# Moving the softmax over slots ahead of the last stage, masking expert rows in the ReLU, six more landing places for expert weights, and a new order of work

## The chip, the core and the metric

The kernel runs on one core of one Trainium2 chip. The core has a matmul engine (TensorE, PE in the profile, with its weight loads shown apart as PEld), a vector engine (VectorE, DVE), an activation engine (ScalarE, ACT), a general engine (GpSimd, POOL) and a sync engine (SyncE, SP), which issues all the DMA transfers here. Each engine runs its own instructions strictly in the order in which they were written, and waits where data or a buffer is not ready. The metric is device time in microseconds, smaller is better.

## The reference

Three parts in a row: attention through 32 memory slots, a max-of-three feed-forward layer, and a soft mixture of 8 experts with 4 slots each. All in float32.

```python
# q, k, v: (8, 8, 576, 64); phi: (8, 8, 576, 32)
a = softmax(phi, over the sequence axis)
k_m = einsum('bhsm,bhsd->bhmd', a, k);  v_m = einsum('bhsm,bhsd->bhmd', a, v)
attn = softmax(q @ k_m.T / 8, axis=-1) @ v_m
x = attn.transpose(0, 2, 1, 3).reshape(4608, 512)
x = maximum(maximum(x @ w1, x @ w2), x @ w3) @ w_out          # 512 -> 768 -> 512
logits = x @ phi2                                              # (4608, 32)
d = softmax(logits, axis=0);  slot_input = d.T @ x             # (32, 512)
for e in range(8): slot_out[e] = maximum(slot_input[e] @ e_w1[e], 0) @ e_w2[e]   # 512 -> 1024 -> 512
c = softmax(logits, axis=1);  out = c @ slot_out
```

The first softmax of the mixture runs over all 4608 tokens and feeds the experts; the second runs over the 32 slots of each token ("the softmax over slots") and is needed only when the output is formed.

## The kernel before, in words

**Main phase.** The kernel treats 8 batches `n`, each with 6 blocks `i` of 128 hidden features: 48 units. A unit needs 6 groups `mn u hf r` (two halves `hf` of the tokens, three weight matrices `r`) of 6 matmuls each, at L641, written into one of three PSUM banks `m`. The function `ev` takes each group out: `r` 0 is a copy on ACT (L651), `r` 1 and 2 are maxima on DVE (L653, L655). Around the groups stand the small steps of the attention: maxima of phi (`mxr`, L426), exponentials, the sums over the sequence (`km`, L477; `kmr`, `kmc`), a transpose (`kvtm`, L501; `kvtc`, L505), scores (`scm`, L516; `sct`, L522), their softmax (`s1r` to `s3l`), and the products of memory and weights (`v1m`, L603; `v1h`, L617; `v1l`, L623). Hidden features are transposed by tokens through DRAM (`trm`, L692; `trc`, L707), multiplied into logits (`lg`, L722) and into running slot sums (`slm`, L789; `sla`, L801). The tokens left over at the end of each batch go the same way in one bundle (`rtm`, L815 and L817; `rtc`, L820; `rsm`). The weights of the feed-forward layer come as 64-bit words and are put together on three engines (`raw`, `cva` at L352, `cvb` at L356, `cvd` at L361, `cvp` at L366).

All of this is one hand-made list, `ORDER`: one pass over it writes the instructions of every engine and every DMA, so the list fixes what stands ahead of what in each engine's queue. `SLOTS` names the buffer that each step takes.

**Expert weights.** They are 64 pieces of 512 KB. `send` issues the next piece into the next of `NSLOT` = 44 places in SBUF; a place that was used is taken again by the piece 44 later. 38 pieces are sent in `ORDER`, the others by the code behind it: one when the main phase ends, one and four more as buffers come free, and the last 20 (44 to 63) while the experts run.

**Last stage.** After `ORDER` come the logits and sums of the last block, the slot inputs (L963 to L995), and the experts: `ex_in` (32 matmul records, L1065), a ReLU on ACT (L1070), `ex_turn` on DVE (a transpose, L1073, and a copy of the expert's four rows into a zeroed buffer `msk`, L1074), `ex_out` for the first half of the output (16 records, L1082). Between the experts, `work[e]` computes the softmax over slots in three pieces (`c_first`, L1020 to L1023; `c_second`, L1029 to L1033) and splits the result into a high part `ch` and a low part `cl`. Then come the 18 output tiles of 512 KB, `st_out` (L1126 to L1138), each with four PSUM copies and a DMA. The first 8 of half 0 alternate with `ex_out(r, 1)`, the second half of the experts' output:

```python
        so_a(0)
        ex_out(0, 1)
        so_b(0)
        for r in range(1, E):
            ex_out(r, 1)
            if r <= NH:
                st_out(r - 1, 0)
        so_a(1)
        st_out(NH, 0)
        so_b(1)
        st_out(NH + 1, 0, True)
```

`warm(n)` issues `n` matmuls that compute nothing, in places where PE would wait; `W` says how many stand at five places of the last stage.

Of the kernel before, what the change touches and what calls it, by code (L numbers as in the profile page):

```python
# [1217 lines left out]
```

## Time and profile before

| | us |
|---|---|
| median of 3 runs | 436.54 (435.85 to 437.97) |
| the profiled execution: its own time | 436.33 |
| the profiled execution: span from the first to the last instruction | 434.6 |

The profiled execution is 0.2 us under the median, and 1.7 us of its time lie outside the span. The granted TensorE clock was 0.991 of full speed over the span. Times below are counted in us from the span's start. Three points order the span: the first of the L641 matmuls at 24.85, the last of them at 363, and the first expert matmul at 378.8.

### The profile page before, as it was taken

The page shows a single profiled execution, that of the slowest core. Times are in us where ns is not written, and L with a number is a line of the kernel's source. Part 1 is how long each engine was busy: PE and PEld are TensorE (multiplying, and loading weights), DVE is VectorE, ACT ScalarE, POOL GpSimd, SP SyncE. Part 2 cuts the span into 40 slices and gives each one's busy share as a digit, 9 for nine tenths or more (in the row PEclk, how much of TensorE's full clock was granted, in tenths as well). Part 3 has the DMA queues.
Part 4 walks back from the last instruction along what each step waited for, and adds up shares of the span by engine and source line. Part 5 has one row for each costly group of instructions (what it writes and reads, how often), then busy time and mean ns, then how long its engine had stood idle before and what let it go on. Part 6 is the DMA issues. An engine that isn't in the chain of part 4 may idle for free.

```text
span 434.6 us, 12284 instructions
## 1 busy us (share of the span) xinstructions
PE 413.8 (95%) x5067; PEld 336.6 (77%) x5067; DVE 313.1 (72%) x731; ACT 182.4 (42%) x430; POOL 88.8 (20%) x102
## 2 busy tenths in 40 slices
PE   8989998999999999999999999999999999999990
PEld 8668787887888879888878798878988888555570
DVE  1597997577988887987599669888866544488480
ACT  3679583644535242344352434334332133132370
POOL 0356633351412011213022212020110000011000
PEclk9999999999999999999999999999999999999996
DMA  8999689928775684672758859468599998599997
GB/s 308 418 414 349 241 322 243 387 83 275 226 177 191 221 307 134 213 286 97 235 190 286 284 194 350 147 196 327 187 293 343 331 314 288 154 410 406 411 399 309
DMA packets 56072, 118.92 MB, mean 274 GB/s; under 512 B 8016, under 2 KB 32336, under 8 KB 53968
## 3 DMA queue, kind: packets, MB, share of 16 engines
q1 hardware_dynamic: 56016, 118.14, 76.9%
q8 instruction: 40, 0.66, 0.6%
q14 instruction: 16, 0.13, 0.1%
HBM read 96.49 MB, written 21.63 MB: 272 GB/s over the span
## 4 chain that ended last, share of the span: by engine, by line
PE 71%; DMA 12%; DVE 9%; ACT 3%; issue 1%; SPq 1%; POOL 1%; DVEq 0%; ACTq 0%; POOLq 0%
PE m L641 44%; DMA arena<-in_w_dram 7%; PE x L603 7%; PE x L477 3%; PE x L789 2%; DMA arena<-in_phi_n_dram 2%; PE m L1065 2%; PE x L1126 2%; PE l L722 2%; PE m L1082 2%; PE x L516 2%; DMA hbuf<-rt 1%; PE l L1082 1%; DMA rt<-arena 1%; DVE vl L623 1%
## 5 line engine op out<-in xcount | busy, mean ns | idle before, releaser
L641 PE MATMUL m<-ah,vh 128*128 128x288 f32 x504 | 147.5, 307 | 1.8 <-DVE g L653 1.1
L641 PE MATMUL m<-ah,vl 128*128 128x288 f32 x504 | 142.1, 296 | 0.0
L641 PEld LDWEIGHTS m<-ah,vh 128*128 128x128 f32 x504 | 94.6, 188 | 20.1 <-issue 11.3
L641 PE MATMUL m<-al,vh 128*128 128x288 f32 x504 | 107.8, 295 | 0.5 <-POOL al L573 0.3
L641 PEld LDWEIGHTS m<-ah,vl 128*128 128x128 f32 x504 | 94.7, 188 | 1.1 <-DVE vl L623 0.8
L641 PEld LDWEIGHTS m<-al,vh 128*128 128x128 f32 x504 | 80.6, 188 | 0.9 <-POOL al L573 0.9
L651 ACT ACTIVATE g<-m 128x288 f32<-128x288 f32 x96 | 39.3, 410 | 91.8 <-PE m L641 88.5
L653 DVE TENSOR_TENSOR g<-m,g 128x288 f32<-128x288 f32 x96 | 42.5, 445 | 26.4 <-PE m L641 16.2
L655 DVE TENSOR_TENSOR ht<-m,g 128x288 f32<-128x288 f32 x96 | 42.3, 451 | 11.6 <-PE m L641 9.1
L617 ACT ACTIVATE vh<-x 128x384 fp32r<-128x384 f32 (+1 forms) x88 | 36.5, 475 | 25.5 <-PE x L603 19.1
L623 DVE TENSOR_TENSOR vl<-x,vh 128x384 fp32r<-128x384 f32 (+1 forms) x88 | 42.5, 524 | 5.5 <-ACT vh L617 5.5
L603 PE MATMUL x<-w,kvt 64*32 64x384 f32 (+1 forms) x800 | 40.0, 477 | 0.9 <-POOL w L366 0.5
L573 POOL TENSOR_TENSOR al<-arena,ah 128x576 fp32r<-128x576 f32 x16 | 23.0, 1435 | 63.4 <-ACT ah L569 56.0
L366 POOL TENSOR_TENSOR w<-w,arena 128x768 uint32<-128x768 uint32 (+1 forms) x13 | 23.6, 1817 | 32.1 <-ACT km L496 15.0
L464 POOL TENSOR_TENSOR arena<-arena,bc 128x640 f32<-128x640 f32 x12 | 19.5, 1637 | 47.1 <-DMA bc<-bcd 22.4
L692 DVE STREAM_TRANSPOSE arena<-ht 128x512 f32<-128x512 f32 x30 | 20.8, 700 | 3.4 <-DMA tr<-arena 2.8
L641 PE MATMUL m<-ah,wh 128*128 128x288 f32 x72 | 21.2, 309 | 0.7 <-DVE ht L655 0.7
L603 PEld LDWEIGHTS x<-w,kvt 64*32 64x32 f32 x800 | 12.0, 105 | 12.3 <-issue 8.1
L641 PE MATMUL m<-ah,wl 128*128 128x288 f32 x72 | 20.2, 295 | 0.0
L801 DVE SCALAR_TENSOR_TENSOR s_run<-s_run,sm,x 128x384 f32<-128x384 f32 (+1 forms) x18 | 10.8, 603 | 9.0 <-PE x L789 9.0
L662 POOL COPY arena<-ht 128x64 f32<-128x64 f32 x24 | 5.3, 236 | 56.2 <-DVE ht L655 55.5
L665 POOL COPY hr_last<-ht 128x64 f32<-128x64 f32 x12 | 3.2, 275 | 66.5 <-DVE ht L655 66.5
(265 smaller groups left out, 649.2 us busy)
## 6 DMA issues: line engine op xcount, KB each, us to landing
arena<-in_e_w_dram SPq DMA_DIRECT2D x33, 512.0 KB, 6.9
arena<-in_w_dram SPq DMA_DIRECT2D x14, 768.0 KB, 7.8
hbuf<-tr SPq DMA_DIRECT2D x42, 256.0 KB, 5.2
arena<-in_kv_dram SPq DMA_DIRECT2D x8, 1290.0 KB, 7.9
arena<-in_q_dram SPq DMA_DIRECT2D x16, 576.0 KB, 7.4
arena<-in_kv_dram SPq DMA_DIRECT2D x8, 1032.0 KB, 7.4
tr<-arena SPq DMA_DIRECT2D x30, 256.0 KB, 2.4
arena<-in_phi_t_dram SPq DMA_DIRECT2D x8, 576.0 KB, 5.8
```

What stands on the lines that cost most here:

```text
L366: (eng or nc.gpsimd).tensor_tensor(out=du, in0=du, in1=lo.bitcast(U32), op=ALU.add)
L464: nc.gpsimd.tensor_tensor(out=x, in0=x, in1=bc_sb[:, :, b].unsqueeze(1).to_broadcast([128, 5, 128]), op=ALU.subtract)
L477: nc.tensor.matmul(t[32 * g:32 * g + 32, 0:KVC], phin_sb[:, j, b, 32 * g:32 * g + 32], kv_sb[:, j, b, g], start=(j == 0), stop=False, tile ...
L573: nc.gpsimd.tensor_tensor(out=al[n][:, :, c], in0=aT_sb[:, :, c], in1=ah[n][:, :, c].bitcast(FP32), op=ALU.subtract)
L603: nc.tensor.matmul(t[b][32 * g:32 * g + 32, 128 * r0:128 * r1], kvt[n][r, b, 32 * g:32 * g + 32], w_v[i][r, g, r0:r1], start=True, stop=Tr ...
L617: nc.scalar.activation(out=v1[n, i][0][:, b, c], in_=ph["v1", n, i, r0][b][:, c], func=ACTF.Copy)
L623: nc.vector.tensor_tensor(out=vl[:, b, c], in0=ph["v1", n, i, r0][b][:, c], in1=vh[:, b, c].bitcast(FP32), op=ALU.subtract)
L641: nc.tensor.matmul(t[:, 0:HALF], x, y, start=(k == 0), stop=(k == 5))
L651: nc.scalar.activation(out=g1[u, hf], in_=t[:, 0:HALF], func=ACTF.Copy)
L653: nc.vector.tensor_tensor(out=g1[u, hf], in0=t[:, 0:HALF], in1=g1[u, hf], op=ALU.max)
L655: nc.vector.tensor_tensor(out=ht[n, i][:, cs], in0=t[:, 0:HALF], in1=g1.pop((u, hf)), op=ALU.max)
L692: nc.vector.transpose(out=v, in_=ht[n, i][:, 0:512])
```

## The change

1. **Softmax over slots.** `c_first` and `c_second` become `c_one` and `c_two`. For the rows of batches 0 to 3 and 4 to 5 they are called from `ORDER` (`ca 0 4`, `cb 0 4`, `ca 4 6`, `cb 4 6`), in SBUF that is free then. Only rows 6 to 8 stay between the experts.
2. **Masked rows.** The ReLU gets a factor per partition, 1 for the rows of its expert and 0 for the others (`own`, in the constants). The transposed rows go straight into the matmul: the buffer `msk`, its clearing and the copy at L1074 are gone.
3. **Low words in place.** `cl` is written over `lt_all`, from which it is made; the outputs' `sh` and `sl` lie in old weight buffers.
4. **Six more places.** `NSLOT` is 50: three places instead of one when the main phase ends, three instead of one in `hbuf`, one of old pieces, one in the room that is left. Pieces 50 to 63 take places 2 to 15 again.
5. **Maxima of phi in rows.** From batch 2 on `mxr` writes the maxima into a 64-column buffer and transposes it, so that the DMA `bcw` writes 8 rows of 32 numbers instead of 256 single ones.
6. **Order.** `ORDER` and `SLOTS` are new throughout, `W` is [1, 0, 0, 2, 1] instead of [1, 0, 0, 3, 2], one `sla` moves behind four small DVE steps (`DEFER`), and `sl_a(L, 0)` goes ahead of three.

```diff
-    "cst; warm 4; phit 0; mxr 0; kv 0 0; pe 0 1; pe 0 0; ptm 0 2; ptc 0 2; ptm 0 1; ptc 0 1; ptm 0 0; ptc 0 0; km "
+    "phit 0; mxr 0; pe 0 0; cst; ptm 0 0; pe 0 1; ptm 0 2; ptm 0 1; warm 4; ptc 0 0; warm 4; kv 0 0; km 0 0 0 2; ptc "
...
+W = [1, 0, 0, 2, 1]
+DEFER = True
...
-NSLOT = EXTRA + 9 + 12 + NX + 6 + 1 + 1 + 2 + 3
+NSLOT = EXTRA + 9 + 12 + NX + 6 + 2 + 3 + 4 + 3 + 1
...
     def slot(k):
-        return slots[k % NSLOT]
+        return slots[k if k < NSLOT else k - NSLOT + 2]
...
+        if n > 1:
+            nc.vector.tensor_reduce(
+                out=pm_sb[:, 0:64].rearrange("p (b x) -> p b x", b=2)[:, :, 0], in_=phit_sb, axis=AX.X, op=ALU.max)
+            nc.vector.transpose(out=pm_sb[:, 64:128], in_=pm_sb[:, 0:64])
+            return
...
+    def c_one(w, m, r0, r1):
+        n = 4 * (r1 - r0)
+        w, m = w[:, 0:32 * n], m[:, 0:n]
+        w3 = w.rearrange("p (x m) -> p x m", m=M)
+        nc.vector.transpose(out=w, in_=lt_all[:, r0:r1].rearrange("p r c -> p (r c)"))
+        nc.vector.tensor_reduce(out=m, in_=w3, axis=AX.X, op=ALU.max)
+        nc.vector.tensor_tensor(out=w3, in0=w3, in1=m.unsqueeze(2).to_broadcast([128, n, M]), op=ALU.subtract)
+        nc.scalar.activation(out=w, in_=w, func=ACTF.Exp)
+
+    def c_two(w, m, r0, r1):
+        n = 4 * (r1 - r0)
+        w, m = w[:, 0:32 * n], m[:, 16:16 + n]
+        w3 = w.rearrange("p (x m) -> p x m", m=M)
+        nc.vector.tensor_reduce(out=m, in_=w3, axis=AX.X, op=ALU.add)
+        nc.vector.tensor_scalar(out=m, in0=m, scalar1=EPS, scalar2=None, op0=ALU.add)
+        nc.vector.reciprocal(out=m, in_=m)
+        nc.vector.tensor_tensor(out=w3, in0=w3, in1=m.unsqueeze(2).to_broadcast([128, n, M]), op=ALU.mult)
+        nc.vector.transpose(out=lt_all[:, r0:r1].rearrange("p r c -> p (r c)"), in_=w)
...
-        more2_sb = more2.tile([128, PIECE], FP32, name="more2")
-        slots.extend(more2_sb[:, PIECE * j:PIECE * j + PIECE] for j in range(1))
-        send(1)
+        more2_sb = more2.tile([128, 3 * PIECE], FP32, name="more2")
+        slots.extend(more2_sb[:, PIECE * j:PIECE * j + PIECE] for j in range(3))
+        send(3)
...
-        msk = hflat[:, 0:2048].rearrange("p (e k g m) -> p e k g m", e=E, k=2, g=4)
-        slots.append(hflat[:, 2048:3072])
-        send(1)
+        slots.extend(hflat[:, PIECE * j:PIECE * j + PIECE] for j in range(3))
+        send(3)
...
-        nc.vector.memset(msk, 0.0)
...
-            nc.scalar.activation(out=h1[e], in_=t[:, 0:256], func=ACTF.Relu)
+            nc.scalar.activation(out=h1[e], in_=t[:, 0:256], func=ACTF.Relu, scale=own[:, e:e + 1])
...
         def ex_turn(e):
-            nc.vector.transpose(out=h_t, in_=h1[e])
-            nc.vector.tensor_copy(
-                out=msk[:, e, :, :, 4 * e:4 * e + 4],
-                in_=h_t.rearrange("p (k g m) -> p k g m", k=2, g=4)[:, :, :, 4 * e:4 * e + 4])
+            nc.vector.transpose(out=h_t[e], in_=h1[e])
...
         work = [
-            lambda: c_first(0, 0, 4), lambda: c_second(0, 0, 4), lambda: c_first(1, 4, 7), lambda: c_second(1, 4, 7),
-            lambda: c_first(0, 7, 9), lambda: c_second(0, 7, 9), c_last1, c_last2,
+            lambda: c_one(cw, cs, 6, 9), lambda: split(0, 4, lt_all[:, 0:4]), c_rest, lambda: split(4, 6, lt_all[:, 4:6]),
+            c_last1, c_last2, lambda: None, lambda: None,
         ]
```

What the new list does is seen in the engines' queues. Three places follow. Line numbers of the change are 6 to 25 higher than those of before.

**ACT at the start, before the first L641 matmul.** In the kernel before, after the two exponentials of phi, the queue holds the first assembly of weights (L352, L356 on `w_55`), the two copies `km`, the copy `kvt` that the first scores need, and then the second assembly:

```order
L352 ACTIVATE w_55<-arena 128x512
L356 ACTIVATE arena<-arena 128x512
L496 ACTIVATE km<-x_154,krs 128x128
L496 ACTIVATE km<-x_171,krs 128x128
L505 ACTIVATE kvt<-x_159 128x256
L352 ACTIVATE w_55<-arena 128x512
L356 ACTIVATE arena<-arena 128x512 x2
```

The same place in the change, where L358 is the L352, L362 the L356, L507 the L496 and L516 the L505 of before:

```order
L358 ACTIVATE w_55<-arena 128x512
L507 ACTIVATE km<-x_176,krs 128x128
L507 ACTIVATE km<-x_150,krs 128x128
L358 ACTIVATE w_55<-arena 128x512
L362 ACTIVATE arena<-arena 128x512
L516 ACTIVATE kvt<-x_159 128x256
L362 ACTIVATE arena<-arena 128x512 x2
```

One step of the first assembly has moved behind `kvt`, and two steps of the second have moved ahead of it.

**SP at the end of the main phase.** `hbuf<-rt` are the loads `rtc`, `hbuf<-tr` the last six loads `trc`, and the rows with `in_e_w_dram` are expert weights. Before:

```order
L329 DMA piece_111<-in_e_w_dram 128x1024
L820 DMA hbuf<-rt 128x4x96 x3
L329 DMA piece_112<-in_e_w_dram 128x1024
L329 DMA piece_113<-in_e_w_dram 128x1024
L820 DMA hbuf<-rt 128x4x96 x3
L329 DMA piece_114<-in_e_w_dram 128x1024
L707 DMA hbuf<-tr 128x4x128 x6
L329 DMA piece_115<-in_e_w_dram 128x1024
L329 DMA piece_116<-in_e_w_dram 128x1024
L329 DMA more_4624<-in_e_w_dram 128x1024
L329 DMA hbuf<-in_e_w_dram 128x1024
```

The change, where the four short rows are one piece (a quarter each), and the pieces number 113 to 118 are the last of `ORDER`:

```order
L831 DMA hbuf<-rt 128x4x96
L335 DMA piece_111<-in_e_w_dram 128x1024
L335 DMA arena<-in_e_w_dram 128x1024
L335 DMA piece_112<-in_e_w_dram 128x1024
L718 DMA hbuf<-tr 128x4x128 x6
L333 DMA bc<-in_e_w_dram 128x256
L333 DMA km<-in_e_w_dram 128x256
L333 DMA kvt<-in_e_w_dram 128x256
L333 DMA more<-in_e_w_dram 128x256
L335 DMA piece_113<-in_e_w_dram 128x1024
L335 DMA piece_114<-in_e_w_dram 128x1024
L335 DMA piece_115<-in_e_w_dram 128x1024
```

The last six loads `trc` now stand ahead of seven pieces of `ORDER`; before, they stood ahead of two.

**DVE in the last third of the main phase, at `sct 7 0`.** The rows with `ht` and `g` are `ev`, those with `vl` are `v1l`. Before:

```order
L655 TENSOR_TENSOR ht_426<-m_367,g_1_489 128x288
L692 STREAM_TRANSPOSE arena<-ht_426 128x512
L522 STREAM_TRANSPOSE arena<-x_171 128x288
L522 STREAM_TRANSPOSE arena<-x_159 128x288
L522 STREAM_TRANSPOSE arena<-x_165 128x288
L522 STREAM_TRANSPOSE arena<-x_154 128x288
```

The change at the same place, where L875 to L879 are `cb 0 4`, L533 is `sct`, and L664 and L666 are the maxima of `ev`:

```order
L666 TENSOR_TENSOR ht_498<-m_390,g_0_424 128x288
L666 TENSOR_TENSOR ht_717<-m_369,g_2_507 128x288
L875 TENSOR_REDUCE cs_e<-arena 128x16
L876 TENSOR_SCALAR cs_e<-cs_e 128x16
L877 RECIPROCAL cs_e<-cs_e 128x16
L878 TENSOR_TENSOR arena<-arena,cs_e 128x512
L879 STREAM_TRANSPOSE lt<-arena 128x512
L533 STREAM_TRANSPOSE arena<-x_176 128x288
L533 STREAM_TRANSPOSE arena<-x_159 128x288
L664 TENSOR_TENSOR g_0_424<-m_369,g_0_424 128x288
```

Five DVE steps of the softmax over slots now stand between one batch of `ev` and the next.

## Rows read from the trace of the kernel before

**Rows 1.** Windows: length, busy of PE, PEld, DVE, ACT, POOL (instructions), clock, DMA share, GB/s.

```profile
25.00:120.00 95.00, 91.43 (x1038) 76.62 (x1042) 75.93 (x159) 58.56 (x115) 41.76 (x34) 1.00 0.77 275
120.00:330.00 210.00, 209.97 (x2563) 176.54 (x2552) 169.62 (x394) 78.36 (x200) 35.35 (x49) 1.00 0.69 231
330.00:363.00 33.00, 31.86 (x268) 28.42 (x268) 15.87 (x38) 8.14 (x23) 1.30 (x6) 1.00 0.95 316
379.00:402.00 23.00, 22.15 (x401) 12.49 (x393) 18.09 (x49) 6.59 (x17) 3.23 (x4) 1.00 1.02 405
```

**Rows 2.** What PE waited for: us in total, times, longest.

```profile
PE m L641 <- DVE g L653: 1.1, 1, 1.1
PE m L641 <- DVE ht L655: 0.7, 1, 0.7
PE x L789 <- DMA hbuf<-rt: 0.4, 1, 0.4
PE l L1082 <- DVE hbuf L1074: 0.9, 2, 0.5
```

**Rows 3.** Timeline of PE around L641: start, us, instruction.

```profile
53.64 0.29 PE L641 MATMUL m<-ah,vl 128*128 128x288 f32 x1
53.77 0.29 PE L641 MATMUL m<-ah,vh 128*128 128x288 f32 x1
```

**Rows 4.** Chain that ended last, around 182, 214, 257, 328: start, us, what.

```profile
181.99 0.65 PE x L603 x16
...
213.93 0.81 PE x L603 x16
...
256.69 7.41 PE m L641 x54
...
328.11 4.43 DMA rt<-arena
```

**Rows 5.** Timeline of ACT and PE at the start.

```profile
15.57 0.38 ACT L505 ACTIVATE kvt<-x 128x256 f32<-128x256 f32 x1 [0.42 <-PE x L501]
15.85 0.66 ACT L352 ACTIVATE w<-arena 128x512 f32<-128x512 f32 x1
16.41 0.70 ACT L356 ACTIVATE arena<-arena 128x512 uint32<-128x512 uint32 x1
...
16.47 0.70 PE L516 MATMUL x<-arena,kvt 64*32 64x288 f32 x16
```

**Rows 6.** Windows of the tile cw (softmax over slots) between the experts.

```profile
sum 18.00, DVE 10.56 ACT 1.57; mean DVE 5.28 ACT 0.79
```

**Rows 7.** Timeline of DVE and ACT before the first expert.

```profile
375.56 1.76 DVE L972 MEMSET hbuf<- 128x2048 f32 x1 [0.48 <-DVE phi L967]
377.24 0.36 DVE L988 COPY s_run<-m 128x256 f32<-128x256 f32 x1
...
376.66 0.38 ACT L987 ACTIVATE s_run<-m 128x256 f32<-128x256 f32 x1 [2.25 <-PE m L978]
```

**Rows 8.** Groups of DVE by form: busy us, mean ns.

```profile
L1074 DVE COPY hbuf<-h_t 128x32 f32<-128x32 f32 x8 | 1.5, 182 | 0.3
```

**Rows 9.** Windows of the DMA in the last stage.

```profile
368.00:374.00 6.00, 5.17 (x59) 2.76 (x57) 3.38 (x14) 1.86 (x7) 0.00 (x0) 1.00 0.25 59
...
417.75:418.50 0.75, 0.75 (x15) 0.63 (x12) 0.70 (x3) 0.73 (x3) 0.00 (x0) 1.00 0.67 268
418.50:431.25 12.75, 5.31 (x84) 4.82 (x82) 5.64 (x17) 5.04 (x16) 0.00 (x0) 0.81 1.02 409
```

**Rows 10.** SP's queue in the last stage.

```profile
417.70 0.33 SPq L1138 DMA_DIRECT2D out_dram<-piece  x1
418.62 0.33 SPq L1138 DMA_DIRECT2D out_dram<-arena  x1
419.28 8.06 SPq L1138 DMA_DIRECT2D out_dram<-piece  x7
427.44 1.09 SPq L1138 DMA_DIRECT2D out_dram<-more  x1
```

More of the change, by code (lines that the diff above doesn't have):

```diff
@@ L254, in mx @@
         return bank(ps_x, "x")
-    cst_sb = keep.tile([128, 388], FP32, name="cst")
+    cst_sb = keep.tile([128, 396], FP32, name="cst")
     ident, ones, sel, grp1 = cst_sb[:, 0:128], cst_sb[:, 128:256], cst_sb[:, 256:384], cst_sb[:, 384:388]
+    own = cst_sb[:, 388:396]
+    cs_e = keep.tile([128, 32], FP32, name="cs_e")
     p_sb = keep.tile([128, NI, M], FP32, name="p")
@@ L261 @@
     wo_sb = keep.tile([128, NI * DM], FP32, name="wo")
-    lt_all = keep.tile([128, 9, 128], FP32, name="lt")
     s_run = keep.tile([128, FF], FP32, name="s_run")
@@ L267 @@
     hbuf = keep.tile([128, 2, 1536], FP32, name="hbuf")
-    bc_sb = keep.tile([128, 128, 2], FP32, name="bc")
+    bc_sb = keep.tile([128, 2, 128], FP32, name="bc")
+    pm_sb = keep.tile([128, 128], FP32, name="pm")
     km_sb = keep.tile([128, 2, 128], FP32, name="km")
@@ L859 @@
         nc.vector.memset(stat[:, 1:2], 0.0)
+        nc.gpsimd.memset(pm_sb, 0.0)
+        mix2 = [s_run[:, 0:256], s_run[:, 256:512]]
         def late_slots_in():
@@ L862, in late_slots_in @@
             more = ctx.enter_context(tc.tile_pool(name="more", bufs=1, side="right"))
-            more_sb = more.tile([128, 6 * PIECE + 256], FP32, name="more")
+            more_sb = more.tile([128, 6 * PIECE + 512], FP32, name="more")
             slots.extend(more_sb[:, PIECE * j:PIECE * j + PIECE] for j in range(6))
-            mix = [bc_sb.rearrange("p c b -> p (c b)"), km_sb.rearrange("p b c -> p (b c)"),
-                   kvt_sb[:, 0].rearrange("p b c -> p (b c)"), more_sb[:, 6 * PIECE:]]
+            mix = [bc_sb.rearrange("p b c -> p (b c)"), km_sb.rearrange("p b c -> p (b c)"),
+                   kvt_sb[:, 0].rearrange("p b c -> p (b c)"), more_sb[:, 6 * PIECE:6 * PIECE + 256]]
+            mix2.extend([more_sb[:, 6 * PIECE + 256:], kvt_sb[:, 1].rearrange("p b c -> p (b c)")])
             slots.extend(late_slots[:6] + [mix] + late_slots[6:])
@@ L992 @@
                 y[:, 32 * k:32 * k + 32], part[:, 128 * k:128 * k + 128], sel[:, 0:M], start=True, stop=True)
+        slots.append(mix2)
+        send(1)
         warm(W[4], True)
@@ L1003 @@
         ch = tail.tile([128, 10, 128], FR, name="ch")
-        cl = tail.tile([128, 10, 128], FR, name="cl")
-        cw = [tail.tile([128, 512], FP32, name="cw%d" % x) for x in range(2)]
-        cs = [tail.tile([128, 32], FP32, name="cs%d" % x) for x in range(2)]
+        cl_a = placed("cl", 9 * 128, FR, lt_at)[0].rearrange("p (x c) -> p x c", x=9)
+        cl_b = tail.tile([128, 1, 128], FR, name="cl_b")
+        cw = tail.tile([128, 384], FP32, name="cw")
+        cs = tail.tile([128, 32], FP32, name="cs")
@@ L1007 @@
         bd = tail.tile([128, 2, 128], FP32, name="bd")
-        sh = tail.tile([128, 512], FR, name="sh")
-        sl = tail.tile([128, 512], FR, name="sl")
-        h_t = tail.tile([128, 256], FP32, name="h_t")
+        sh, sl = (placed(x, 512, FR, w_at + 4 * (2 * PIECE + 512 * j))[0] for j, x in enumerate(("sh", "sl")))
+        slots.append(tail.tile([128, PIECE], FP32, name="last"))
+        send(1)
         def split(x0, x1, src):
             nc.scalar.activation(out=ch[:, x0:x1], in_=src, func=ACTF.Copy)
-            nc.gpsimd.tensor_tensor(out=cl[:, x0:x1], in0=src, in1=ch[:, x0:x1].bitcast(FP32), op=ALU.subtract)
@@ L1025, in c_second @@
-        def c_second(k, r0, r1):
-            n = 4 * (r1 - r0)
-            w, m = cw[k % 2][:, 0:32 * n], cs[k % 2][:, 16:16 + n]
-            w3 = w.rearrange("p (x m) -> p x m", m=M)
-            nc.vector.tensor_reduce(out=m, in_=w3, axis=AX.X, op=ALU.add)
-            nc.vector.tensor_scalar(out=m, in0=m, scalar1=EPS, scalar2=None, op0=ALU.add)
-            nc.vector.reciprocal(out=m, in_=m)
-            nc.vector.tensor_tensor(out=w3, in0=w3, in1=m.unsqueeze(2).to_broadcast([128, n, M]), op=ALU.mult)
-            nc.vector.transpose(out=lt_all[:, r0:r1].rearrange("p r c -> p (r c)"), in_=w)
-            split(r0, r1, lt_all[:, r0:r1])
+            nc.gpsimd.tensor_tensor(out=cl_b if x0 == 9 else cl_a[:, x0:x1], in0=src, in1=ch[:, x0:x1].bitcast(FP32), op=ALU.subtract)
@@ L1037, in c_last1, with c_rest @@
+        def c_rest():
+            c_two(cw, cs, 6, 9)
+            split(6, 9, lt_all[:, 6:9])
         def c_last1():
@@ L1057 @@
         h1 = {}
+        h_t = [slots[e // 4][:, 256 * (e % 4):256 * (e % 4) + 256] for e in range(E)]
         h1_sb = [h5l[:, 256 * j:256 * j + 256] for j in range(2)]
@@ L1082, in ex_out @@
                     nc.tensor.matmul(
-                        acc[x][32 * g:32 * g + 32, 0:256], msk[:, e, k, g],
+                        acc[x][32 * g:32 * g + 32, 0:256], h_t[e][:, 128 * k + 32 * g:128 * k + 32 * g + 32],
                         part_of(k0 + k, g),
@@ L1109, in so_b @@
             nc.vector.tensor_tensor(out=sl[:, c], in0=t[:, 0:256], in1=sh[:, c].bitcast(FP32), op=ALU.subtract)
-        free = [slots[64 - NSLOT + j] for j in range(NSLOT - (64 - NSLOT))]
-        free = [x for x in free if not isinstance(x, list)]
+        free = [slots[j] for j in range(66 - NSLOT, NSLOT)]
+        free = [x for x in free if not isinstance(x, list) and x is not w_late[2]]
         def st_out(r, x, pool=None):
@@ L1120, in st_out @@
                 ts = [mx() for _ in range(4)]
-            for k, (c, o) in enumerate(((ch, sh), (cl, sh), (ch, sl))):
+            for k, (c, o) in enumerate(((ch, sh), (cl_a, sh), (ch, sl))):
                 for g in range(4):
@@ L1128, in st_out @@
             if r == 8:
-                for k, (c, o) in enumerate(((ch, sh), (cl, sh), (ch, sl))):
-                    nc.tensor.matmul(ts[3][:, 0:256], c[:, 9], o[:, cs], start=(k == 0), stop=(k == 2))
+                for k, (c, o) in enumerate(((ch, sh), (cl_a, sh), (ch, sl))):
+                    nc.tensor.matmul(ts[3][:, 0:256], cl_b[:, 0] if k == 1 else c[:, 9], o[:, cs], start=(k == 0), stop=(k == 2))
             tok = free.pop(0)
@@ L1197 @@
     cst[:, 384:388] = _np.repeat(_np.eye(4), 32, 0)
+    cst[:, 388:396] = _np.tile(_np.repeat(_np.eye(E), 4, 0), (4, 1))
     nc = _bacc.Bacc("TRN2", target_bir_lowering=False, num_devices=1, dynamic_dma_scratch_size=512)
```

59 lines of the change are left out of this document (30 added, 29 removed), and 257 rows, old and new, of the table ORDER.

## Prediction

> **What bounds the kernel now.** I read the windows by stage first, then what PE waited for, then the timelines, and last the DMA of the last stage. From 120 to 330 us PE is busy 209.97 of 210.00 us, from 25 to 120 it lacks 3.57 us, from 330 to 363 it lacks 1.14 [rows 1]. DVE is busy 169.62 of 210 us beside it, 81%, and PE never waits for it there. So the main phase is a queue of PE work of fixed length: it ends where its first L641 group begins, plus the work, plus some 4.7 us of waits (3.57 + 0.03 + 1.14). The waits I can name are one behind DVE of 1.1 us, one of 0.7 us in 330 to 363, and one of 0.4 us for a load `rtc` [rows 2].
>
> That "busy" is real pace is seen in the starts: L641 records follow each other every 0.13 us (53.64, 53.77) [rows 3], and a run of 54 takes 7.41 us, 0.137 each, at 257 us as well [rows 4]. The Trainium skill (Perfetto Trace Analysis, Identifying the Most-Contended Engine) calls matmul busy time a bad measure and asks for the busy share of weight loads. By that, 176.54 of 210 us [rows 1], PE would have 16% to spare and a new order could win tens of us; a new order changes no matmul's own 0.13 us, so I count this only as a reason to give the list rival below its chance.
>
> The last stage has two limits that lie close together. DMA moves 405 GB/s at a share of 1.02 from 379 to 402 [rows 1], which looks like a bound. But at 417.75 to 418.5 its share falls to 0.67 and then is 1.02 until 431.25 [rows 9]. SP issues an output at 417.70, and then nine more [rows 10]. The ten outputs take 12.75 us, 1.28 each, and they fill the whole stretch to the end [rows 9]. So the queue had caught up at 418: the end is set by the moment at which output nine (row 8 of half 0) was ready, not by the weights. That moment hangs on PE: ReLU, turn, expert matmuls, then eight turns of `ex_out` and `st_out`.
>
> **The change, part by part.** The count of matmuls in the list is the same but for warm ones, so what can move is the start, the switches between kinds, the waits, and the last stage.
>
> *Start.* In the queue of ACT, `kvt` ran at 15.57, before the second assembly at 15.85 and 16.41 [rows 5]. Now L358 and L362, the same two steps, stand ahead of it: 0.56 us from start to start and 0.70 for the second, some 1.26 us. One step of the first assembly has gone behind `kvt`, which gives back at most 0.57, but `km` then waits for DVE's reciprocal anyway. The scores at 16.47 had 0.52 us of slack behind the end of `kvt` (15.57 + 0.38) [rows 5]. So the scores, and with them the chain of DVE and ACT steps up to the first L641 group, come between 0.2 (1.26 - 0.57 - 0.52) and 0.74 us later (1.26 - 0.52). I take 0.55, near the upper end, because of that reciprocal. All PE work follows: **+0.55**.
>
> *Runs.* In PE's queue the L641 matmuls stand in 55 runs instead of 49. Counted by sixths of the 288 groups, the sixths change by +1, +1, -1, +2, 0 and +3, so nearly all new switches lie where PE has no wait to hide them. A `v1m` of 16 records takes 0.81 us between two runs and 0.65 beside another small step, 0.16 more; a run of 54 takes 0.21 us more than 54 times 0.133 [rows 4]. Bounds: nothing, if a run takes the place of a wait, and 0.37, if both hold. I take 0.18, between the two rows: six runs, **+1.1** (0 to 2.2).
>
> *Softmax over slots.* DVE spent 10.56 us on the tile `cw` between the experts [rows 6]; six of nine row blocks move, about 7.0 us, into a stretch where DVE is 81% busy. Seven us over the 100 us in which the four calls stand make that some 88%. I cost it at nothing: the work that hides it is PE's, two to three L641 groups of 0.8 us that can run into the three `m` banks while DVE is away. Without that cover it costs what the third rival says.
>
> *Maxima in rows, own column, low words.* `mxr`, `bcw` and `bc_s` feed the sums of a batch that PE reaches much later; in 120 to 330 PE waited for none of them [rows 1]. Nothing, either way; the cover is the same 0.03 us of idle.
>
> *Waits at the end of the main phase.* The 0.7 us came from a transpose `rtm` that waited for a DMA of 4.43 us [rows 4] while DMA was at a share of 0.95 [rows 1]. The change sends 16 expert pieces instead of 20 between group 242 and the last, but leaves the same two groups between the two `rtm` that share a buffer. And its `rsm` comes three groups earlier, which needs the loads `rtc` earlier too. Between nothing and the whole 1.14 us I take half: **-0.55**.
>
> *Before the experts.* Without the clearing of `msk` (1.76 us), DVE's L988 can start with ACT's L987 at 376.66 instead of 377.24 [rows 7], 0.58 us; one warm step fewer stands in PE's way. **-0.5** (0 to 0.6).
>
> *Experts.* PE waited 0.9 us in two places for the copy L1074 [rows 2]. The first wait was behind the big softmax steps, which are gone (0.46); the second loses the copy itself, 0.18 [rows 8]. **-0.65** (0.2 to 0.9). The rest of PE's 22.15 of 23 us [rows 1] is matmuls, as many as before.
>
> *Six places.* DMA stands at a share of 0.25 from 368 to 374 [rows 9]: 4.5 us that more places can fill with loads. Two more pieces go at the end of the main phase, two more into `hbuf`, two behind that, and only 14 instead of 20 wait for an expert to free a place. Against that, seven pieces of the list, not two, now stand behind the last loads `trc`. Since output nine, not the weights, sets the end, I cost all of it at **nothing**. The cover is the queue being empty at 418; without it the second rival's price holds.
>
> **Sum.** 436.33 (the profiled execution; 0.2 under the median of 436.54) + 0.55 + 1.1 - 0.55 - 0.5 - 0.65 = 436.28, so 436.3: no change that can be told. A measurement of this kernel tells about 0.5%, 2.2 us, from no change.
>
> **Rivals.** *The list packs PE better* (chance 0.20). Of the 4.7 us of waits in 25 to 363, the new order removes 3.5, and the new runs fall into waits: 436.33 + 0.55 - 3.5 - 1.15 = 432.2. For it: nearly all of the idle lies before 120, where orders differ most. Against: the same kind of wait (a transpose behind a transfer of `trm`, behind raw weights) stands at the same groups in the new list.
>
> *The last stage is bound by its queue* (0.12). Then the idle 4.5 us [rows 9] are filled, on top of the last stage's 1.15: 436.33 - 4.5 - 1.15 + 0.55 = 431.2. The same section of the Trainium skill's Perfetto Trace Analysis says to judge DMA by the bandwidth that it uses and to work on the most contended engine first; by that the last stage at 405 GB/s is a DMA stage, and earlier loads pay. The share of 0.67 at 417.75 [rows 9] speaks against it: whoever is late there has no transfer left to wait for.
>
> *PE waits behind the softmax steps on DVE* (0.22, the other side). `cb 0 4` is five steps in a row, two thirds of a softmax of 512 columns: by its share of the 10.56 us [rows 6] some 2.4 us; `ca 0 4` some 2.1, the other two 1.2 and 1.5. Behind each stand maxima that free `m` banks, and two L641 groups cover 1.6 us. If one maximum of 0.45 must follow before a bank is free, the four cost 1.25, 0.95, 0.05 and 0.35, together 2.6; the sum becomes 438.9, and 440 with the upper end of the runs. It decides where fewer than two free groups stand behind a call.
>
> *The change does nothing there*: places are free earlier but SP, which issues in order, holds the loads behind `trc` until late. That gives the forecast's time and is part of it.
>
> **Chances.** The forecast, within 434.4 to 438.7: 0.46. Faster by over 0.5%: 0.32 (the two rivals 0.20 and 0.12). Slower by over 0.5%: 0.22. The two faster rivals give 432.2 and 431.2, the slower one 438.9 to 440; each with half a us of its own, the range is 431 to 440.2.
>
> **What would show it.** First L641 group near 25.4 instead of 24.85. PE still lacking under 0.3 us in 120 to 330; a wait of L641 for a DVE maximum right behind L875 to L879 would mean the third rival. Between the first expert matmul and the last group of half 0, no wait for DVE over 0.3 us. The DMA share: no dip to 0.25 after the main phase, but dips between the first eight outputs, and the last ten outputs again back to back, 12.8 us; if there is no dip at all until the end, the second rival is right. The prediction is wrong if the start of the main phase or its waits move by more than 2 us, which no row of before can exclude, since the list is new throughout.

## The result and the profile after

The changed kernel takes **431.22 us** (430.25 to 433.4, 4 runs) against 436.81 in the same session, a ratio of **0.9878, 95% interval 0.9832 to 0.9923**. Six more runs of it later gave 0.9849 (0.9812 to 0.9887). It is 1.2 to 1.5% faster. That lies inside the range, but only 0.2 us from its faster end, and in part by luck: the range reaches 431 because of the queue rival's 431.2, which is not what came, while the list rival with its half a us ends at 431.7. The likeliest case, no change, was wrong by 5 us. The profiled execution took 430.85 us, its span is 429.1 instead of 434.6.

The windows of the changed kernel by stage, and around the last outputs (columns as in [rows 1]):

```profile
25.00:120.00 95.00, 93.66 (x1112) 78.89 (x1114) 76.89 (x171) 60.29 (x117) 42.27 (x35) 1.00 0.82 298
120.00:330.00 210.00, 209.96 (x2489) 177.29 (x2480) 173.44 (x400) 80.39 (x203) 37.15 (x52) 1.00 0.67 219
330.00:363.00 33.00, 33.00 (x345) 28.92 (x337) 18.96 (x49) 8.25 (x25) 1.13 (x5) 1.00 0.95 312
379.00:402.00 23.00, 22.73 (x410) 12.91 (x406) 9.97 (x27) 6.85 (x18) 3.48 (x4) 1.00 1.03 404
...
363.00:369.00 6.00, 5.08 (x106) 2.59 (x95) 3.16 (x15) 2.61 (x8) 0.00 (x0) 1.00 1.02 408
412.00:414.00 2.00, 2.00 (x43) 1.78 (x39) 1.84 (x6) 1.43 (x5) 0.00 (x0) 1.00 0.81 324
414.00:426.00 12.00, 4.43 (x70) 4.02 (x69) 4.77 (x14) 4.32 (x14) 0.00 (x0) 0.80 1.02 404
```

Against [rows 1], PE lacks 1.34 us instead of 3.57 in 25 to 120, and nothing instead of 1.14 in 330 to 363. From 120 to 330 nothing changed, and the 3.8 us more of DVE's work there delayed no one. The DMA gap behind the main phase [rows 9] is gone, the dip before the last ten outputs (0.81) is still there. Four of PE's rows divide the span (start, us, instruction): the first feed-forward group, the closing logits, the first expert, and the first matmul of `so_b`, where the outputs begin. Before, they stood at 24.85, 367.22, 378.76 and 401.90.

```profile
25.29 0.40 PE L652 MATMUL m<-ah,vh 128*128 128x288 f32 x1
362.98 0.43 PE L842 MATMUL l<-hr_last,p 128*32 128x32 f32 x28
374.35 0.85 PE L1090 MATMUL m<-extra,p 128*32 128x256 f32 x12
396.54 0.70 PE L1130 MATMUL x<-h5l,cst 128*128 128x256 f32 x2
```

So the main phase, from the first row to the second, is 4.68 us shorter (342.37 to 337.69). It starts 0.44 later; the way to the first expert is 0.17 shorter, the experts 0.95, and the outputs to the end of the span 0.1. That is the 5.5 us. What PE waited for from 25 to 366 us, all of it (us in total, times, longest; the last two stand behind the closing logits):

```profile
PE m L652 <- POOL al L584: 0.7, 1, 0.7
PE x L461 <- ACT arena L454: 0.3, 1, 0.3
PE x L952 <- DVE fin L944: 0.2, 1, 0.2
PE x L785 <- DVE s_run L812: 0.2, 1, 0.2
```

None of the waits that [rows 2] names in the main phase is left, and none stands behind the softmax calls.

### The profile page after: what moved, and what is told of

It reads as the page before. It is cut to its first block, busy times and chain, and to the rows that moved or that the text cites. A ratio compares the mean times of both kernels' runs of the same rounds, so it can differ in the third digit from the quotient of the medians.

```text
span 429.1 us, 12282 instructions
## 1 busy us (share of the span) xinstructions
PE 410.8 (96%) x5061; PEld 335.6 (78%) x5061; DVE 308.6 (72%) x728; ACT 183.2 (43%) x431; POOL 90.5 (21%) x103
## 4 chain that ended last, share of the span: by engine, by line
PE 86%; DMA 5%; DVE 5%; ACT 1%; issue 1%; SPq 1%; DVEq 0%; ACTq 0%
PE m L652 53%; PE x L614 8%; PE m L1090 3%; DMA arena<-in_q_dram 3%; PE x L488 3%; PE x L800 3%; PE l L733 2%; PE x L1149 2%; PE x L527 2%; PE m L1105 2%; DMA tr<-extra 2%; PE l L1105 1%; PE x L381 1%; DVE vl L634 1%; PE x L699 1%
## 5 line engine op out<-in xcount | busy, mean ns | idle before, releaser
L664 DVE TENSOR_TENSOR g<-m,g 128x288 f32<-128x288 f32 x96 | 42.5, 444 | 31.4 <-PE m L652 22.0
L666 DVE TENSOR_TENSOR ht<-m,g 128x288 f32<-128x288 f32 x96 | 42.7, 452 | 16.1 <-PE m L652 13.7
L628 ACT ACTIVATE vh<-x 128x384 fp32r<-128x384 f32 (+1 forms) x88 | 36.8, 475 | 31.4 <-PE x L614 25.3
L475 POOL TENSOR_TENSOR arena<-arena,bc 128x640 f32<-128x640 f32 x12 | 18.6, 1569 | 33.1 <-PE m L652 13.2
L614 PEld LDWEIGHTS x<-w,kvt 64*32 64x32 f32 x800 | 11.1, 105 | 13.1 <-issue 8.7
L673 POOL COPY arena<-ht 128x64 f32<-128x64 f32 x24 | 7.9, 341 | 61.7 <-DVE ht L666 61.6
L556 ACT ACTIVATE arena<-arena 128x576 f32<-128x576 f32 x16 | 10.9, 682 | 15.6 <-DVE arena L552 15.6
L488 PE MATMUL x<-arena 128*32 128x129 f32 x512 | 16.4, 274 | 0.5 <-DMA arena<-in_kv_dram 0.5
```

The lines of the kernel that those rows point to most:

```text
L475: nc.gpsimd.tensor_tensor(out=x, in0=x, in1=bc_sb[:, b].unsqueeze(1).to_broadcast([128, 5, 128]), op=ALU.subtract)
L488: nc.tensor.matmul(t[32 * g:32 * g + 32, 0:KVC], phin_sb[:, j, b, 32 * g:32 * g + 32], kv_sb[:, j, b, g], start=(j == 0), stop=False, tile ...
L614: nc.tensor.matmul(t[b][32 * g:32 * g + 32, 128 * r0:128 * r1], kvt[n][r, b, 32 * g:32 * g + 32], w_v[i][r, g, r0:r1], start=True, stop=Tr ...
L628: nc.scalar.activation(out=v1[n, i][0][:, b, c], in_=ph["v1", n, i, r0][b][:, c], func=ACTF.Copy)
L664: nc.vector.tensor_tensor(out=g1[u, hf], in0=t[:, 0:HALF], in1=g1[u, hf], op=ALU.max)
L666: nc.vector.tensor_tensor(out=ht[n, i][:, cs], in0=t[:, 0:HALF], in1=g1.pop((u, hf)), op=ALU.max)
```

## The experiments

My theory after this: the *list* took the time, by PE's waits and by its switches. Rivals: the *queue* (the six places fill the DMA gap and that pays), the *softmax steps* (the move frees the experts), and, after the first four runs, the *rows* (the phi maxima). One table holds what each run measured. "Main" is PE's time from the first feed-forward group to the closing logits; "waits" the listed waits in it; "rest" is main less waits, that is matmuls with their switches and with stalls too short to be listed. The next columns go from the closing logits to the first expert and from there to `so_b`.

| kernel | ratio (95%) | first group | main | waits | rest | to expert | to `so_b` | span |
|---|---|---|---|---|---|---|---|---|
| before | 1 | 24.85 | 342.37 | 4.47 | 337.90 | 11.54 | 23.14 | 434.6 |
| before, again | | 24.71 | 342.82 | 4.91 | 337.91 | 11.53 | 23.16 | 435.0 |
| change | 0.9878 (0.983 to 0.992) | 25.29 | 337.69 | 1.01 | 336.68 | 11.37 | 22.19 | 429.1 |
| change, again | 0.9849 (0.981 to 0.989) | 24.18 | 338.19 | 1.54 | 336.65 | 11.38 | 22.19 | 428.4 |
| e1 old list | 0.9971 (0.994 to 1.000) | 25.23 | 340.40 | 2.85 | 337.55 | 11.29 | 23.57 | 433.3 |
| e2 no places | 0.9877 (0.983 to 0.993) | 23.79 | 338.94 | 2.18 | 336.76 | 11.37 | 22.20 | 430.5 |
| e3 softmax late | 0.9862 (0.983 to 0.990) | 24.93 | 338.52 | 1.91 | 336.61 | 11.37 | 23.56 | 430.9 |
| e4 list alone | 0.9945 (0.992 to 0.997) | 24.57 | 341.24 | 4.75 | 336.49 | 11.62 | 23.20 | 433.4 |
| e6 more runs | 1.0076 (1.005 to 1.011) | 25.56 | 346.52 | 2.85 | 343.67 | 11.37 | 22.20 | 438.2 |
| e7 start | 0.9890 (0.984 to 0.994) | 29.16 | 337.03 | 0.68 | 336.35 | 11.37 | 22.20 | 432.9 |
| e8 rows alone | 0.9982 (0.995 to 1.001) | 24.89 | 341.94 | 3.92 | 338.02 | 11.53 | 23.15 | 434.2 |
| e9 single numbers | 0.9950 (0.992 to 0.998) | 25.57 | 339.61 | 2.81 | 336.80 | 11.37 | 22.20 | 431.1 |
| e10 copy back | 0.9892 (0.986 to 0.992) | 25.18 | 337.82 | 1.01 | 336.81 | 11.48 | 22.32 | 429.6 |
| e11 fewer runs | 0.9985 (0.996 to 1.001) | 25.11 | 344.05 | 5.45 | 338.60 | 11.37 | 22.20 | 435.3 |

The column "rest" repeats within 0.2 us for one list, so differences above that can be read; "waits" and "first group" move by 1 to 1.5 us from run to run.

**The old list in the changed kernel (e1).**

```diff
-ORDER, SLOTS of the change
+ORDER, SLOTS of before
-            lambda: c_one(cw, cs, 6, 9), lambda: split(0, 4, lt_all[:, 0:4]), c_rest, lambda: split(4, 6, lt_all[:, 4:6]),
-            c_last1, c_last2, lambda: None, lambda: None,
+            lambda: c_one(cw, cs, 0, 3), lambda: c_rest(0, 3), lambda: c_one(cw, cs, 3, 6), lambda: c_rest(3, 6),
+            lambda: c_one(cw, cs, 6, 9), lambda: c_rest(6, 9), c_last1, c_last2,
```

`DEFER` and the logits step behind the list are those of before as well.

> The changed kernel with the order of work and the buffer list of the kernel before; all nine rows of the softmax over slots are then computed between the experts, in three pieces of three rows; masked rows, low words in place, phi maxima in rows and the six places stay. List theory (the 5.5 us come from PE's waits and switches in the main phase, and 1.1 from the masked rows): the last group of the feed-forward matmuls again near 363, the first expert matmul near 378.6, time 436.8 - 1.1 = 435.7. Queue theory (the last stage is bound by its DMA queue and the six places pay): the DMA gap after the main phase is filled although the main phase is as long as before, 431 to 432.

Measured: 0.9971, or 435.5 us by the 436.8 of before. For this list the queue theory falls: the DMA share in 360 to 376 rises to 0.88 from 0.65, but the time stays far from the 431 to 432 of that theory. The rest is nearly that of before, but the waits are 1.6 to 2.1 lower, which I had not expected of the edits that were left.

**Without the six places (e2).**

```diff
-NSLOT = EXTRA + 9 + 12 + NX + 6 + 2 + 3 + 4 + 3 + 1
+NSLOT = EXTRA + 9 + 12 + NX + 6 + 1 + 1 + 2 + 3
```

> The changed kernel with 44 places instead of 50. List theory: same time as the changed kernel, 431.2, within 0.5, because output nine and not the weights sets the end; a gap of some 4 us in the DMA comes back behind the main phase. Queue theory: the gap comes back, and since this list sends five pieces fewer before the last feed-forward group, the weights bind: 3 to 4.5 us more, 434.5 to 435.5, with PE waiting for weights between the experts and no dip of the DMA share before the end.

Measured: 0.9877, as the change. Part of the gap is back (369 to 376 us, 250 GB/s; the change has 404 there):

```profile
369.00:376.00 7.00, 6.92 (x86) 5.13 (x89) 1.35 (x5) 0.91 (x3) 0.00 (x0) 1.00 0.82 250
```

But now the dip before the last ten outputs is missing, a sign that the expectation gave to the queue theory. The rows are of e2, then of the change:

```profile
408.00:414.00 6.00, 5.15 (x77) 3.98 (x73) 4.38 (x12) 3.58 (x12) 0.00 (x0) 1.00 1.02 413
```

```profile
408.00:414.00 6.00, 5.16 (x77) 3.99 (x69) 4.60 (x13) 3.79 (x12) 0.00 (x0) 1.00 0.91 364
```

So with this list and 44 places the DMA queue never runs empty there (e10, also with 44, has 1.03 in that stretch). From PE's last matmul to the end of the span e2 takes 11.8 us, the change 10.7, e10 10.9; from `so_b` it is 34.2, 32.5 and 32.8. With this list the places are worth 0.2 to 1.7 us in these profiles, which the ratios cannot tell from nothing.

**All softmax between the experts (e3).** `ca` and `cb` leave the list; `work` as in e1.

> The changed kernel with all of the softmax over slots between the experts again, in three pieces of three rows; list otherwise the same. List theory: DVE has room in both places, so the main phase is the same (last group near 360.7) and between the experts PE waits at most 0.5 us more: 431.2 to 431.8. Theory that moving it pays: some 7 us more of DVE work beside 23 us of experts where DVE is already at 14 to 18 us make it a bound, PE waits behind DVE there by 1 us or more, 432.3 or above. Theory that the move cost something in the main phase: 0.5 us or more faster than the changed kernel.

Measured: the main phase is that of the change, so the four calls cost nothing in it. Between the experts PE needs 23.56 instead of 22.19 us: 0.7 instead of 0.3 in the one listed wait (below), the rest in time that no listed wait shows. Against three pieces of three rows, moving the softmax gives **1.4 us** there; before, which cut it into 4, 3 and 2 rows, needed 23.14 with the copy. The time (0.9862) can't tell that from the change.

```profile
PE l L1107 <- DVE extra L1101: 0.7, 1, 0.7
```

**The new list alone (e4).** The kernel before with the new `ORDER` (without `ca`, `cb`) and `SLOTS`, and with the two steps behind the list that go with it (`lt_m(5, 6)`, `sl_a(6, 1)`).

> The kernel before with the new order of work and buffer list alone (its softmax calls left out of the list, so all of it stays between the experts as before); 44 places, the copy into msk and phi maxima as single numbers as before. List theory: the main phase ends 4.2 us earlier as in the changed kernel, the rest is as before, 432.5. Queue theory: five pieces fewer are sent before the last group and there are no more places, so the gain of the main phase is lost in a DMA-bound last stage: 435 to 437.

Measured: 0.9945, some two fifths of what the change gives, and not for the queue's reason. The rest fell by 1.4, but the waits stayed, at other places. What PE waited for from 25 to 366 us, the largest:

```profile
PE m L643 <- DVE g L655: 3.4, 2, 2.2
PE m L643 <- POOL al L575: 0.7, 1, 0.7
```

Ahead of the 2.2 us DVE stood 3.19 us before a transpose into `extra`, whose earlier content was still on its way out; in the change the same step stood 1.06 us. The rows are of e4, then of the change:

```profile
81.88 0.71 DVE L694 STREAM_TRANSPOSE extra<-ht 128x512 f32<-128x512 f32 x1 [3.19 <-DMA tr<-extra]
```

```profile
80.74 0.71 DVE L703 STREAM_TRANSPOSE extra<-ht 128x512 f32<-128x512 f32 x1 [1.06 <-DMA tr<-extra]
```

So list and code seem to work together, and the part of the code that I suspected is the write of the phi maxima. The next two runs change it alone, both ways.

**Rows alone (e8), and the change with single numbers (e9).**

```diff
-        nc.sync.dma_start(out=t.rearrange("o (p b) -> (o p) b", b=2), in_=ph["pmax", n][:, 0:2])
+        nc.sync.dma_start(
+            out=t.rearrange("o (b a x) -> (o a) b x", a=4, b=2),
+            in_=pm_sb[:, 64:128].rearrange("(a j) (b x) -> a j b x", a=4, b=2)[:, 0])
```

> The kernel before with one edit alone, the phi maxima in rows of 32 numbers from batch 2 on. If the waits at 73 and 76 us came from transfers that stood behind the 256 single numbers, the waits behind the maxima (1.1) and behind the copies on ACT (0.7) are gone, and the main phase is 1.6 to 2.0 us shorter: 434.8 to 435.2. By the prediction, which costed this edit at nothing, 436.8 and both waits still there.

> The changed kernel with that one edit undone: phi maxima written as 256 single numbers. If the new list needs the rows, PE waits behind DVE for some 3.4 us between 70 and 120 us, as in the kernel before with the new list alone, and the time is 434.6. By the prediction (nothing either way) 431.2, and no wait over 1 us in 25 to 120.

Measured in e8: 0.9982, 0.8 us with an interval that holds zero. The place is right, the size is not. Here are the windows of before, where the write was issued at 64.21, and its DVE:

```profile
66.00:68.00 2.00, 2.00 (x34) 1.60 (x33) 1.87 (x5) 1.33 (x2) 1.45 (x2) 1.00 1.32 214
68.00:70.00 2.00, 2.00 (x17) 2.00 (x16) 1.49 (x2) 0.70 (x2) 1.30 (x3) 1.00 0.40 57
```

```profile
72.07 0.71 DVE L692 STREAM_TRANSPOSE extra<-ht 128x512 f32<-128x512 f32 x1 [2.25 <-DMA tr<-extra]
```

The same in e8:

```profile
66.00:68.00 2.00, 2.00 (x34) 1.63 (x33) 1.87 (x5) 1.24 (x2) 1.45 (x2) 1.00 0.78 222
68.00:70.00 2.00, 2.00 (x18) 2.00 (x17) 1.69 (x3) 0.78 (x2) 1.24 (x3) 1.00 0.99 332
```

```profile
69.66 0.70 DVE L700 STREAM_TRANSPOSE extra<-ht 128x512 f32<-128x512 f32 x1
```

Over these four us the DMA share is the same in the mean (0.86, in e8 0.88; a window counts the whole of a packet that starts in it, so one of them can exceed 1), but behind the single numbers only half as much flows: 136 instead of 277 GB/s. In rows the transpose runs 2.4 us earlier, and both of PE's waits at 73 and 76 are gone. The second profile of before (203 and 73 GB/s) and e1 with its rows (231 and 283) show the same. Why the small pieces hold up those behind them, no run shows. The time gains little because other waits grew: 0.8 behind ACT at 113 is new, and the load `rtc` at 356 costs 1.1 instead of 0.4; the one at 332 stayed (0.5, before 0.7). (What is written singly are 128 pairs, not 256 numbers: for each of six batches the trace of before has 128 packets of 8 bytes, that of e8 8 of 128.) The Trainium skill (DMA: Bandwidth & Descriptors, Specifications) asks for at least 512 B in a transfer for full rate. These runs agree that pieces of 8 bytes are costly; the figure itself they do not test, since the rows of 128 bytes lie below it too.

Measured in e9: 0.995, slower than the change by 2.1 us by the spans and by 3 to 4 by the ratios (its profiled execution is the fastest of its twelve); its waits are 1.8 us longer than in the change's first profile. At 82 us, where e4 lost 2.2, PE waits only 0.4:

```profile
81.29 0.71 DVE L697 STREAM_TRANSPOSE extra<-ht 128x512 f32<-128x512 f32 x1 [1.36 <-DMA tr<-extra]
```

So the single numbers do not explain e4's longest wait; what does stays open. Its other one, 1.2 us at 115, is in e9 too, and in no profile of this list with rows. It begins in SP's queue. The rows are of e9, then of the change:

```profile
89.63 0.96 SPq L440 DMA_DIRECT2D bcd<-pmax  x1
...
97.50 0.32 SPq L443 DMA_DIRECT2D bc<-bcd  x1
...
98.80 0.33 SPq L421 DMA_DIRECT2D arena<-in_phi_n_dram  x1
```

```profile
89.32 0.55 SPq L444 DMA_DIRECT2D bcd<-pm  x1
...
94.42 0.32 SPq L449 DMA_DIRECT2D bc<-bcd  x1
...
95.74 0.33 SPq L421 DMA_DIRECT2D arena<-in_phi_n_dram  x1
```

SP holds the load of the maxima until their write has landed, 7.9 us after its issue instead of 5.1, and the load of phi behind it comes 3.1 us later. What SP waited for in this way in all, in e9 and in the change:

```profile
SPq L443 <- DMA bcd<-pmax: 15.6, 3, 6.3
```

```profile
SPq L449 <- DMA bcd<-pm: 8.9, 3, 4.4
```

Before has no such wait: its list issues each of these loads 12 us or more behind the write. So the new list needs the rows more than the old one. What follows at 115 is seen in DVE and POOL of e9:

```profile
105.48 3.65 POOL L469 TENSOR_TENSOR arena<-arena,bc 128x640 f32<-128x640 f32 x2 [14.91 <-DMA arena<-in_phi_n_dram]
...
106.06 1.63 DVE L546 TENSOR_TENSOR arena<-arena,smax 128x576 f32<-128x576 f32 x1
...
107.98 1.76 DVE L546 TENSOR_TENSOR arena<-arena,smax 128x576 f32<-128x576 f32 x1
```

POOL's subtraction waited for that late load, and so it ran beside DVE's two, which took 1.63 and 1.76 us instead of their median of 0.75. In the change POOL does it from 101.94 to 105.03, before DVE comes to them.

**Plain ReLU and the copy (e10).** On top of e2:

```diff
-            nc.scalar.activation(out=h1[e], in_=t[:, 0:256], func=ACTF.Relu, scale=own[:, e:e + 1])
+            nc.scalar.activation(out=h1[e], in_=t[:, 0:256], func=ACTF.Relu)
...
+        nc.vector.memset(msk, 0.0)
...
+            nc.vector.tensor_copy(
+                out=msk[:, e, :, :, 4 * e:4 * e + 4],
+                in_=h_t[e].rearrange("p (k g m) -> p k g m", k=2, g=4)[:, :, :, 4 * e:4 * e + 4])
```

> The changed kernel with 44 places, and the masked rows undone: plain ReLU, a zeroed buffer, and the copy of the expert's four rows behind each transpose. The softmax over slots stays in the main phase. Prediction's terms: 0.5 us more before the first expert (the clearing of 1.76 us stands ahead of a copy on DVE) and 0.2 to 0.65 more between the experts (0.18 for each copy that PE waits for): 432.0 to 432.4. If masking is worth nothing: the same times from the last logits to the first expert (11.4) and from there to the outputs (22.2) as without the copy.

Measured: 0.11 us more to the first expert, 0.12 between the experts. Masking is worth **0.2 us**, not the 0.7 to 1.1 expected.

**More runs (e6) and fewer (e11).** In e6 16 logits steps stand behind the next group; in e11 five small steps stand some groups later, where the next small step is.

```diff
-lg 2 0; lg 2 1; hrc 14; ... mn 17 0 1;
+lg 2 0; hrc 14; ... mn 17 0 1; lg 2 1;
```

> The changed kernel with 16 places of its list changed between groups 90 and 245: where logits steps stand side by side, the later ones move behind the next feed-forward group, so PE's queue has 71 instead of 55 runs of feed-forward matmuls and 15 more runs of logits, with the same matmuls. By the prediction's price of 0.18 for a run, 2.9 us for the 16 runs, and as much again if the logits runs count too: PE's time from the first group to the last logits 2.9 to 5.7 us longer, 434 to 437. By what I read from the changed kernel's own runs since (0.12 for a feed-forward run, 0.11 for a logits run), 3.5 us. If a run costs nothing while PE's queue is full, no change.

> The changed kernel with five small steps of its list moved behind the next few feed-forward groups, where the next small step stands: 50 instead of 55 runs of feed-forward matmuls, the same matmuls. At the 0.23 us for a run that the kernel with more runs showed, PE's time from the first group to the last logits without its waits falls from 336.7 by some 1.1 us; at nothing for a run it stays. The time can tell little of it: 430.0 to 431.2.

Measured in e6: 2% slower than the change. The rest grows by 7.0 us: 3.5 in the feed-forward matmuls (16 more runs, 0.22 each), 2.4 in the logits (15 more, 0.16 each; 8 records between two groups take 0.35, beside another small step 0.22), 1.1 elsewhere. Waits add 1.8. Measured in e11: five runs fewer, and the rest does not fall by 1.1 but grows by 1.9, the waits by 4.4. What PE waited for there:

```profile
PE x L617 <- DVE vl L637: 1.2, 1, 1.2
PE m L655 <- DVE g L667: 1.1, 1, 1.1
PE m L655 <- ACT g L665: 0.9, 2, 0.5
PE x L491 <- issue: 0.8, 1, 0.8
```

The feed-forward matmuls took 242.4 us, as with 55 runs. So counting runs does not price a list: a `v1m` that comes four groups late (236.3 us) makes ACT's and DVE's steps behind it late, and from 234 to 243 us PE waits 3.1 us in three places, where the change waits for nothing.

**The start (e7).** `q 0 0` ahead of `raw 0`, and `kvtm 0; kvtc 0` ahead of `cvb 0`.

> The changed kernel with two steps moved at the start of its list: the load of the first queries ahead of the second load of raw weights, and the copy kvt ahead of the last step of the first assembly. By the prediction's start term (all PE work follows the first group) the end of the main phase moves with the first group, some 0.5 to 0.9 us earlier. By what the runs with the new list show (first groups from 23.8 to 25.3, last groups all near 360.9), an earlier first group is waited away later, and the end of the main phase moves by under 0.3 us.

Measured: it went the other way. The raw weights came later, POOL's assembly with them (18.67 instead of 16.38), the scores ran at 18.03 instead of 17.03, and the first group at 29.16. The rows are of e7, the last one of the change:

```profile
20.02 0.45 PE L617 MATMUL x<-w,kvt 64*32 64x128 f32 x16 [1.27 <-POOL w L375]
...
21.88 3.78 PE L862 MATMUL l<-cst 128*128 128x128 f32 x14
...
29.16 0.38 PE L655 MATMUL m<-ah,vh 128*128 128x288 f32 x1
```

```profile
15.00:20.00 5.00, 2.53 (x29) 1.61 (x29) 1.89 (x5) 2.95 (x6) 1.33 (x2) 1.00 1.02 416
20.00:25.00 5.00, 4.80 (x48) 3.71 (x49) 4.88 (x11) 3.30 (x8) 3.09 (x3) 0.60 1.03 426
```

```profile
19.38 2.15 PE L859 MATMUL l<-cst 128*128 128x128 f32 x14
```

Only 1 to 2 us of the lateness stand at the scores, where the edit acts. The rest is the clock: in this profile the granted TensorE clock fell to the lower of its two levels (1.2 instead of 2.4 GHz) at 21 us, when PE had been busy for 2.53 of the 5 us before 20 (4.25 in the change), and rose again at 28; no other profile here has that at the start. The 14 `warm` matmuls took 3.78 us instead of 2.15, the scores and `warm` steps behind them 2.6 instead of 1.7, most of the other 2.9 us. The profiled execution is also the longest of its four (434.72; the others 431.3 to 432.3, against 430.2 to 431.8 of the change in the same session). Of the 3.9 to 5.0 us by which its first group is later than in the change's two profiles, 3.2 to 3.8 arrive at the closing logits. So some four fifths of a later start are passed on; an earlier one, as e2's at 23.79, was given back in waits (2.18).

**Both kernels again (e12, e13).** Unchanged.

> The kernel before, unchanged, for a second profile. If the list's gain lies in the waits and the switches, PE's time from the first group to the last logits again holds some 338 us without the listed waits, against 336.7 with the new list, and its waits are again 3 us or more; if the waits differ from run to run as much as between the lists, they may be as low as the 1 to 2.2 us of the new list.

> The changed kernel, unchanged, in more rounds: a ratio of 0.985 to 0.990, waits of PE in the main phase of 1 to 2.2 us, and 336.7 us without them.

Measured: as expected. Of before PE waits 4.5 and 4.9 us, the same rest to 0.01 us; of the change's list with rows five profiles (the change twice, e2, e3, e10) have waits of 1.0 to 2.2, 1.5 in the mean, and a rest of 336.6 to 336.8. No version was better than the change.

## Why the prediction was wrong about the main phase and, in sum, right about the rest

Two terms make nearly all of the miss of 5.4 us by the spans: the runs (+1.1 forecast, -1.2 measured) and the waits (-0.55 forecast, -3.5 measured). The prediction's own sign of being wrong, waits that move by more than 2 us, came.

**The bound** was named rightly: the main phase is PE's queue, and what it gains arrives at the end. The end is still set by the moment at which the last ten outputs are ready.

**Start, +0.55.** In the profiled pair +0.44, and the second assembly stands ahead of `kvt` as forecast. But in this profile the scores then waited for the load of the queries, not for `kvt`:

```profile
15.06 0.67 ACT L358 ACTIVATE w<-arena 128x512 f32<-128x512 f32 x1
15.63 0.67 ACT L362 ACTIVATE arena<-arena 128x512 uint32<-128x512 uint32 x1
16.20 0.36 ACT L516 ACTIVATE kvt<-x 128x256 f32<-128x256 f32 x1
...
17.03 0.72 PE L527 MATMUL x<-arena,kvt 64*32 64x288 f32 x16 [0.59 <-DMA arena<-in_q_dram]
```

Over five profiles of this list the first group lies between 23.8 and 25.3, 24.7 in the mean, where before has 24.7 and 24.9. These profiles show no shift. In three of them the scores waited for the queries, and the first group came at 24.9 to 25.3; in two (the change again, e2) they waited 0.2 for `kvt`, and it came at 24.2 and 23.8.

**Runs, +1.1.** This step failed in its sign: the rest fell by **1.2**. The feed-forward matmuls did pay, 0.35 us for six runs more (0.6 against the second profile of before). But the prediction counted only their runs. The small steps gave more back: logits 0.8 and slot sums 0.6, which alternate in fewer and longer runs now (34 instead of 40), `kvt` and `dt` 0.3 each. All of it is pieces of 0.1 to 0.3 us that no list of waits shows; they were not tried one by one.

**Maxima in rows, nothing.** This step failed, and it failed in its reason: "PE waited for none of them" was read from 120 to 330 us, where nothing waits at all, while the transfers that the single numbers hold up stand at 66 to 116 us. In the new list the rows are worth 2 us or more (e9), in the old one 0.4 to 0.9 by the main phase and 0.8 by the ratio, which can't be told from nothing (e8). Nor did the prediction ask what stands behind that write in SP's queue, which is where the new list pays for it.

**Waits, -0.55.** This is the largest error: the waits fell by 3.5 in the profiled pair, by 3.2 in the mean of the profiles. The prediction took half of the idle at the end of the main phase and left the 3.57 us before 120 to a rival of 0.20. That rival (*the list packs PE better*, 432.2) is the case that came, with this amendment: the list alone (e4) removes no waiting. List and rows remove it together; of e4's waits the one of 2.2 us at 82 is not explained by the rows (e9).

**Softmax over slots, nothing in the main phase:** right. In the experts its move gives 0.8 (change against before, less the mask) to 1.4 (e3), of which the prediction saw 0.46, booked under the copy.

**Before the experts, -0.5:** measured -0.17. The clearing held DVE's copy for only 0.17 us. Without it the copy starts not with ACT's, as forecast, but when ACT's is done, 0.41 us behind its start (before 0.58):

```profile
372.44 0.38 ACT L1025 ACTIVATE s_run<-m 128x256 f32<-128x256 f32 x1 [2.25 <-PE m L1016]
...
372.85 0.42 DVE L1026 COPY s_run<-m 128x256 f32<-128x256 f32 x1 [1.99 <-ACT s_run L1025]
```

**Experts, -0.65:** measured -0.95, with the shares changed: the softmax 0.8 or more, the mask 0.1. The two terms together, -1.15, came out at -1.12; that they match is luck.

**Six places, nothing:** right, to within 1.7 us. But the reason given, a queue that is empty before the last ten outputs, holds for the new list only with the places; without them the dip is missing (e2, e10). The 4.5 us of idle DMA were filled for the greater part by the pieces that the new list sends later: 31 instead of 36 stand ahead of the last feed-forward group (369 to 376 us: before 83 GB/s, e2 250, the change 404).
